# First expert block: order of fetches, routing steps and one-hots

## The chip, the cores and the metric

The kernel runs on one core of a Trainium2 chip. The metric is the device time of one execution in microseconds (us); what is given for the kernel before is the median of three timed runs.

## The reference

Attention with a sigmoid in place of the softmax, then a mixture of experts with one expert per token and a skip rule, then a dense two-layer network, all in float32:

```python
# q, k, v: (4, 12, 448, 64)
scores = np.matmul(q, k.transpose(0, 1, 3, 2)) / np.sqrt(64) - np.log(448)
x = np.matmul(1 / (1 + np.exp(-scores)), v)      # then (1792, 768): token, 12 heads * 64
# experts: w_skip (768), w_gate (768, 8), w1 (8, 768, 1024), w2 (8, 1024, 768)
run = x @ w_skip > 0                             # the other tokens pass unchanged
e_idx = np.argmax(x[run] @ w_gate, axis=1)
gate_w = softmax(x[run] @ w_gate)[e_idx]
x[run] += gate_w * (np.maximum(x[run] @ w1[e_idx], 0) @ w2[e_idx])
# dense: w_in (768, 2048), w_out (2048, 768)
h = x @ w_in
out = np.where(h > 0, h, np.exp(np.minimum(h, 0)) - 1) @ w_out
```

## The kernel before

**Products.** A float32 factor is kept as a high and a low part: ScalarE (ACT) casts the high part, VectorE (DVE) subtracts it to get the low part, and `gemm` makes three matmuls of the two pairs. For weights `split_w` does this, the cast `whi` on ACT and the subtraction `wlo` on DVE, 128 x 1536 at a time.

**Stages.** Attention goes in 24 steps of two heads (`scores` and mixing, matmuls `ps` and `po`) and leaves x transposed in `xT`. The experts work on blocks of 256 tokens; which tokens stand in a block is data. Block 0 is special: its tokens come from the first ten 128-row tiles alone (SOON = 10), so that its routing (`sooner`) is done during the last attention steps. Its rows are gathered from the copy of x in DRAM, `x_d`, by two indirect DMAs of GpSimd (`gather_first`), 128 rows each, as soon as the slot table `inv` has been turned into `slot_0`. Blocks 1 and on wait for the routing of all 14 tiles.

**Block 0's weights.** An expert's weights are 8 chunks of 768 KB, c0 to c3 of w1 and c4 to c7 of w2. `fetch` issues them on the SP queue, which runs in program order: c0 and c1 one step before the end of attention, c2 and c3 when the last step begins, c4 and c5 right behind attention, c6 and c7 when c0 and c1 have been split, since they take their buffers (NRAW0 = 6). Two chunks at a time are held as split pairs ahead of use: `ahead(i, c)` splits chunk c + 2.

**The product of block 0.** `first_block` is one generator-driven program. `columns` flips the gathered rows on TensorE (PE) and splits them into `x2` (`both` in the trace). Then come 16 calls of `up_one(0, c, f)`, chunk c (0 to 3) and column group f (0 to 3), which build h; after c = 1 and c = 3 `h_one` makes h's high part on ACT and its low part on DVE. After each `up_one` the generator `routing` is advanced by one step, up to its next `yield`; this is how the routing of the last four tiles and the order of all further blocks are woven into block 0's products. Chunks c4 to c7 follow (`back`), with four routing steps after each, then `slot_order`, twelve small matmuls that use twelve `one_hot` tiles and the offsets `ca`.

**The late row tiles.** The first steps of `routing` also write the last four tiles of x to `x_d`: `rows(t)` for t = LATE to LATE + 3 (10 to 13). Each has six flips on PE into two PSUM banks (always the same two, `acc2` and `acc4`), two ACT copies into a row buffer `xr`, and one write on the SP queue. There are two buffers `xr`, so the copies of one tile need the write of the tile two before it, and the flips of the next tile need the banks that these copies read.

**The routing chain.** After the late tiles' choices (`choose`, `positions`) DVE computes the first slot of every expert, every token's slot, one-hots of slots (`rt_tok`, in `spots`), and block kinds. PE multiplies these: `ordered` and `inv` (which gives `slot_tok`, by which block 1 is gathered), `kn` and `ig`; then DVE makes `kinds`, from which PE loads the branch of block 1, and the twelve one-hots (`order_rows`).

What sets the order on each engine is the order in which these Python functions issue the instructions; engines run in program order and meet through semaphores.

Of the kernel before, what the change touches and what calls it, by code (L numbers as in the profile page):

```python
# [91 lines left out]
def build(nc, tc, a):  # L92
# [3 lines left out]
    with ExitStack() as top:  # L96
# [80 lines left out]
        with ExitStack() as st:  # L177
# [250 lines left out]
            def sooner():  # L428
# [55 lines left out]
                gather_first()  # L484

            whi_t, wlo_t = [], []

# [8 lines left out]
            def raw_of(i, c):  # L496
                return raw_t[(8 * i + c) % NRAW if i else c % NRAW0]

            def fetch(i, chunks):
                if i == NB:  # L500
                    return
                e = nc.values_load(
                    blk_e[i : i + 1, :1] if i else blk_0[:1],
                    engines=[mybir.EngineType.SP], min_val=0, max_val=E - 1,
                )
                for c in chunks:
                    src = (w1, w2)[c // 4][bass.ds(e, 1), c % 4].rearrange("o p f -> (o p) f")
                    nc.sync.dma_start(raw_of(i, c), src)

            def gather(i, late=True):  # L510
                at = slot_ext if late else slot_tok
                for h in range(2):
# [7 lines left out]
                    )  # L520

            def gather_first():
                for h in range(2):
                    nc.gpsimd.indirect_dma_start(
                        out=xg_t[0][h][:],
                        out_offset=None,
                        in_=x_d[: SOON * P, :],
                        in_offset=bass.IndirectOffsetOnAxis(ap=slot_0[:, h : h + 1], axis=0),
                        bounds_check=SOON * P - 1,
                        oob_is_err=False,  # L530
                    )

# [84 lines left out]
            for n in range(steps + 1):  # L617
# [5 lines left out]
                if n == steps:  # L623
                    qst.close()
                    wi1p = top.enter_context(tc.tile_pool(name="wi1p", reuse_waits="tile", bufs=1))
                    wi1 = wi1p.tile([P, DM], F32, name="wi1")
                    tokp = st.enter_context(tc.tile_pool(name="tokp", reuse_waits="tile", bufs=1))
                    some_weights(tokp, 2, 2)
                    fetch(0, range(2, 4))
                    lg = logits(B - 1, None, range(KD - 2))  # L630
# [59 lines left out]
            assert done_rows == LATE and narrowed == 2 * FA  # L690
            columns(0, [pss.tile([P, 2, 512], F32, name="pc", tag="ps")[:, 0] for _ in range(3)])
            logits(B - 1, lg, range(KD - 2, KD))
            ast.close()
# [38 lines left out]
            def routing():  # L732
# [9 lines left out]
                yield  # L742
                rows(LATE + 1, banks)
                pos, cnt = positions(SOON, NTT, acc_t[5])
                nc.vector.scalar_tensor_tensor(
                    ni, cnt, float(BLK - 1), took[:, 0], op0=ALU.add, op1=ALU.subtract
# [13 lines left out]
                nc.vector.reduce_sum(span[:, 0], tmp, axis=AX.X)  # L760
                yield
                rows(LATE + 2, banks)
                nc.vector.scalar_tensor_tensor(
# [3 lines left out]
                nc.vector.reduce_sum(fv, fo, axis=AX.X)  # L767
                yield
                rows(LATE + 3, banks)
                run(places(SOON, NTT, pos))  # L770
                nc.gpsimd.tensor_add(posk[:, late], posv[:, late], skip[:, late])
                yield
# [6 lines left out]
                    aa, sa.to_broadcast([P, NTT, NHB]), grid("iota_a", NTT, NHB), op=ALU.is_equal  # L779
                )  # L780
                yield
                run(spots(SOON, NTT, slot_i[:, late]))
                yield
                nc.vector.tensor_add(span[:, 1], span[:, 0], nb[:, 0])
# [4 lines left out]
                with nc.allow_low_precision("whole numbers up to 14"):  # L789
                    nc.vector.reduce_sum(blk_e, own, axis=AX.XY)  # L790
                yield
                ordered = acc_t[2][:, :E1]
# [184 lines left out]
            def first_block(aside):  # L977

                for c in range(4):
                    nh, c3 = divmod(c, 2)  # L980
                    for f in range(4):
                        up_one(0, c, f)
                        next(aside, None)
                        if c3:
                            h_one(4 * nh + f)
                        if f == 2:
                            ahead(0, c)
                ahead(0, 4)
                for c in range(4, 8):
                    if c == 5:  # L990
                        ahead(0, 5)
                    back(0, 1, P, range(c, c + 1))
                    for _ in range(4):
                        next(aside, None)
                outcome(0, 1, P)
                run(aside)
                back(0, 0, P, range(4, 5))
                slot_order()
# [142 lines left out]
            def order_rows():  # L1141
                for t in range(NOR):
                    nc.vector.tensor_scalar(
                        one_hot[0][:, t], iota_h, cr[:, t], None, op0=ALU.is_equal
                    )
# [310 lines left out]
```

## Time and profile before

| | |
|---|---|
| median of three runs | 918.95 us (917.61 to 919.28) |
| profiled execution, its own time | 919.79 us |
| its span, first to last instruction | 918.0 us |
| PE (matmul) busy | 887.1 us, 97% |
| DVE busy | 557.7 us, 61% |
| ACT busy | 485.3 us, 53% |
| POOL (GpSimd) busy | 75.6 us, 8% |
| DMA engines, mean rate | 147 GB/s |

The busy times are sums over the whole span. Time outside the span (919.79 - 918.0) is start and end of the program. The block that is changed lies from about 160 to 215 us of the span.

### The profile page before, as it was taken

The numbers are of one execution on the slowest core, as the hardware profiler recorded it, in microseconds if no ns is written. First come the engines' busy times: TensorE is split into PE (matmuls) and PEld (weight loads), VectorE is DVE, ScalarE is ACT, GpSimd is POOL, SyncE is SP. The second block draws the span as 40 slices with busy tenths as digits, with TensorE's granted clock in tenths as the row PEclk, the third lists the DMA queues.
The fourth block names the chain that finished last, engine by engine and source line by source line (L and its number), as shares of the span: only waits on it lengthen the run. The fifth ranks groups of instructions, "written<-read, shape, count | busy, mean of one in ns | idle before, by whom it ended". The sixth has DMA issues, their size and how long they took to land.

```text
span 918.0 us, 13615 instructions
## 1 busy us (share of the span) xinstructions
PE 887.1 (97%) x5208; PEld 714.6 (78%) x5208; DVE 557.7 (61%) x872; ACT 485.3 (53%) x679; POOL 75.6 (8%) x76
## 2 busy tenths in 40 slices
PE   9999999889999897999899999999999999999998
PEld 4445545589999786888688888888888888888997
DVE  2968678478566375786688886533443543443664
ACT  7777776453455463674445544444443444444664
POOL 1000000113101032221100000100000100000100
PEclk9999999999999999899999999999999999999999
DMA  8788875659947084964553431100100100000100
GB/s 286 253 278 281 297 268 208 262 163 411 391 159 278 13 318 179 409 221 145 203 160 87 123 115 41 69 1 1 35 18 18 69 1 1 0 1 10 61 1 35
DMA packets 34196, 134.73 MB, mean 147 GB/s; under 512 B 4698, under 2 KB 5850, under 8 KB 34098
## 3 DMA queue, kind: packets, MB, share of 16 engines
q1 hardware_dynamic: 29474, 114.22, 35.0%
q0 software_dynamic: 4480, 19.01, 5.8%
q8 instruction: 57, 0.93, 0.4%
q14 instruction: 41, 0.34, 0.1%
q10 hardware_dynamic: 144, 0.23, 0.1%
HBM read 112.47 MB, written 23.99 MB: 149 GB/s over the span
## 4 chain that ended last, share of the span: by engine, by line
PE 91%; DVE 3%; ACT 2%; issue 2%; DMA 1%; POOL 0%; DVEq 0%; ACTq 0%; POOLq 0%
PE acc L1331 16%; PE pt L1331 10%; PE acc L1298 8%; PE acc L1299 8%; PE acc L1300 8%; PE po L256 8%; PE ps L242 7%; PE acc L549 5%; PE acc L548 5%; PE acc L550 5%; PE acc L142 1%; PE acc L907 1%; PE acc L908 1%; DVE wlo L541 1%; PE pt L142 1%
## 5 line engine op out<-in xcount | busy, mean ns | idle before, releaser
L541 DVE TENSOR_TENSOR wlo<-raw,whi 128x1536 fp32r<-128x1536 f32 x64 | 111.3, 1756 | 31.8 <-ACT whi L539 31.2
L1307 ACT ACTIVATE m<-acc 128x512 f32<-128x512 f32 (+1 forms) x64 | 34.9, 545 | 177.2 <-PE acc L1300 167.0
L1309 DVE SCALAR_TENSOR_TENSOR m<-m,acc 128x512 f32<-128x512 f32 (+1 forms) x64 | 39.8, 621 | 143.7 <-ACT m L1308 143.7
L539 ACT CAST whi<-raw 128x1536 fp32r<-128x1536 f32 x64 | 93.8, 1481 | 21.8 <-PE acc L550 8.8
L249 ACT ACTIVATE at<-ps,bias 112x896 f32<-112x896 f32 x96 | 88.9, 1011 | 24.9 <-PE ps L242 24.5
L1331 PE MATMUL acc<-wol,gh 128*128 128x256 f32 x320 | 100.7, 315 | 0.0
L1331 PE MATMUL acc<-woh,gl 128*128 128x256 f32 x320 | 100.4, 314 | 0.0
L1331 PE MATMUL acc<-woh,gh 128*128 128x256 f32 x320 | 100.4, 314 | 0.0
L1299 PE MATMUL acc<-x,wih 128*128 128x512 f32 (+1 forms) x270 | 96.2, 356 | 0.0
L1298 PE MATMUL acc<-x,wih 128*128 128x512 f32 (+1 forms) x270 | 96.2, 356 | 0.0
L1300 PE MATMUL acc<-x,wil 128*128 128x512 f32 (+1 forms) x270 | 96.1, 356 | 0.0
L549 PE MATMUL acc<-wlo,both 128*128 128x384 f32 (+1 forms) x236 | 84.0, 356 | 4.1 <-issue 3.7
L548 PE MATMUL acc<-whi,both 128*128 128x384 f32 (+1 forms) x236 | 84.8, 359 | 0.0
L550 PE MATMUL acc<-whi,both 128*128 128x384 f32 (+1 forms) x236 | 83.5, 354 | 0.0
L256 PE MATMUL po<-at,vt 112*64 112x448 f32 x384 | 77.5, 545 | 0.0
L1287 DVE TENSOR_TENSOR wol<-wo,woh 128x768 fp32r<-128x768 f32 x64 | 61.2, 957 | 23.3 <-ACT woh L1286 23.0
L1331 PEld LDWEIGHTS acc<-woh,gh 128*128 128x128 f32 x320 | 60.3, 188 | 9.9
L1331 PEld LDWEIGHTS acc<-wol,gh 128*128 128x128 f32 x320 | 60.3, 188 | 9.4
L1286 ACT CAST woh<-wo 128x768 fp32r<-128x768 f32 x64 | 53.3, 833 | 25.9 <-PE acc L1331 25.8
L1313 DVE TENSOR_TENSOR gl<-m,gh 128x512 fp32r<-128x512 f32 (+1 forms) x64 | 40.1, 626 | 40.5 <-ACT gh L1312 40.5
L1331 PEld LDWEIGHTS acc<-woh,gl 128*128 128x128 f32 x320 | 60.1, 188 | 4.2
L1281 DVE TENSOR_TENSOR wil<-wi,wih 128x768 fp32r<-128x768 f32 x60 | 57.4, 957 | 6.7 <-ACT wih L1280 6.0
(261 smaller groups left out, 1876.0 us busy)
## 6 DMA issues: line engine op xcount, KB each, us to landing
raw<-in_w SPq DMA_DIRECT2D x66, 768.0 KB, 7.9
raw<-in_wi SPq DMA_DIRECT2D x9, 768.0 KB, 6.3
raw<-in_wo SPq DMA_DIRECT2D x9, 768.0 KB, 6.8
vt<-in_v SPq DMA_DIRECT2D x12, 448.0 KB, 5.4
x_d<-xr SPq DMA_DIRECT2D x14, 384.0 KB, 5.4
raw<-in_wi SPq DMA_DIRECT2D x14, 384.0 KB, 3.1
raw<-in_wo SPq DMA_DIRECT2D x14, 384.0 KB, 3.1
qr<-in_q SPq DMA_DIRECT2D x11, 448.0 KB, 4.8
```

The costliest lines, as they stand in the source:

```text
L242: nc.tensor.matmul(ps[:CP, j, :S], kk[head, p, c * CP : (c + 1) * CP], qq[head, p], start=(i == 0), stop=(i == 2),)
L249: nc.scalar.activation(at[:, :, c, :], ps[:CP, :, :S], AF.Sigmoid, bias=bias[:CP], scale=QK_SCALE)
L256: nc.tensor.matmul(po[64 * j : 64 * j + 64, :S], vt[:, 2 * (hp % 2) + j, c, :], at[:, j, c, :], start=(c == 0), stop=(c == NCH - 1),)
L539: nc.scalar.copy(w_hi, raw)
L541: nc.vector.tensor_sub(w_lo, raw, w_hi)
L548: nc.tensor.matmul(o, a_hi, b_hi, start=first, stop=False)
L549: nc.tensor.matmul(o, a_hi, b_lo, start=False, stop=False)
L550: nc.tensor.matmul(o, a_lo, b_hi, start=False, stop=last)
L1298: nc.tensor.matmul(o, a, b, start=(cc == 0), stop=False)
L1299: nc.tensor.matmul(o, a, c, start=False, stop=False)
L1300: nc.tensor.matmul(o, wil[:, cc], b, start=False, stop=(cc == KD - 1))
L1331: nc.tensor.matmul(o, a, b, start=(clears and f == 0 and k_ == 0), stop=(f == KF2 - 1 and k_ == 2), skip_group_check=True,)
```

## The change

Six edits. `fetch` of c2 and c3 gets a dependency on both gathers of `gather_first`. A one-element Exp on ACT stands behind `columns` (the function table for Exp is loaded there). The steps of `routing` are regrouped: DVE work moves to earlier steps, `rows(LATE + 1)` to `rows(LATE + 3)` stand later within their step, and two steps fewer are left ahead of `ordered`. The splits of c2 to c5 are issued behind `up_one` (1, 0), (1, 2), (2, 2) and (3, 2), where they were issued behind (0, 2), (1, 2), (2, 2) and (3, 2). The twelve `one_hot` instructions go from DVE to GpSimd. The load of the dense weights `wi1`, whose line is unchanged, comes out at another place.

```diff
@@ -483,6 +483,9 @@
                 nc.vector.tensor_scalar_add(slot_0, inv, float(NT))
                 gather_first()
 
+            SYNC = mybir.DependencyInfo(
+                mybir.DependencyClass.Sync, mybir.DependencyReason.DATA
+            )
             whi_t, wlo_t = [], []
 
             def some_weights(pool, raws, splits):
@@ -496,7 +499,7 @@
             def raw_of(i, c):
                 return raw_t[(8 * i + c) % NRAW if i else c % NRAW0]
 
-            def fetch(i, chunks):
+            def fetch(i, chunks, after=()):
                 if i == NB:
                     return
                 e = nc.values_load(
@@ -505,7 +508,9 @@
                 )
                 for c in chunks:
                     src = (w1, w2)[c // 4][bass.ds(e, 1), c % 4].rearrange("o p f -> (o p) f")
-                    nc.sync.dma_start(raw_of(i, c), src)
+                    dma = nc.sync.dma_start(raw_of(i, c), src)
+                    for other in after:
+                        tc.add_manual_dep(dma.ins, other.ins.name, SYNC)
 
             def gather(i, late=True):
                 at = slot_ext if late else slot_tok
@@ -519,16 +524,18 @@
                         ),
                     )
 
+            first_rows = []
+
             def gather_first():
                 for h in range(2):
-                    nc.gpsimd.indirect_dma_start(
+                    first_rows.append(nc.gpsimd.indirect_dma_start(
                         out=xg_t[0][h][:],
                         out_offset=None,
                         in_=x_d[: SOON * P, :],
                         in_offset=bass.IndirectOffsetOnAxis(ap=slot_0[:, h : h + 1], axis=0),
                         bounds_check=SOON * P - 1,
                         oob_is_err=False,
-                    )
+                    ))
 
             def split_w(i, c, hi=True, lo=True):
                 if i == NB:
@@ -626,7 +633,7 @@
                     wi1 = wi1p.tile([P, DM], F32, name="wi1")
                     tokp = st.enter_context(tc.tile_pool(name="tokp", reuse_waits="tile", bufs=1))
                     some_weights(tokp, 2, 2)
-                    fetch(0, range(2, 4))
+                    fetch(0, range(2, 4), first_rows)
                     lg = logits(B - 1, None, range(KD - 2))
                 if p == 0 and n < steps:
                     if n:
@@ -689,6 +696,7 @@
             run(soon)
             assert done_rows == LATE and narrowed == 2 * FA
             columns(0, [pss.tile([P, 2, 512], F32, name="pc", tag="ps")[:, 0] for _ in range(3)])
+            nc.scalar.activation(warm, bias, AF.Exp)
             logits(B - 1, lg, range(KD - 2, KD))
             ast.close()
             pst.close()
@@ -740,8 +748,9 @@
                 fetch(0, range(NRAW0, 8))
                 rows(LATE, banks)
                 yield
-                rows(LATE + 1, banks)
                 pos, cnt = positions(SOON, NTT, acc_t[5])
+                run(places(SOON, NTT, pos))
+                nc.gpsimd.tensor_add(posk[:, late], posv[:, late], skip[:, late])
                 nc.vector.scalar_tensor_tensor(
                     ni, cnt, float(BLK - 1), took[:, 0], op0=ALU.add, op1=ALU.subtract
                 )
@@ -758,17 +767,12 @@
                 )
                 nc.vector.tensor_mul(tmp, nb.to_broadcast([P, E, E]), first)
                 nc.vector.reduce_sum(span[:, 0], tmp, axis=AX.X)
-                yield
-                rows(LATE + 2, banks)
                 nc.vector.scalar_tensor_tensor(
                     base[:, 0], span[:, 0], float(BLK), took[:, 0], op0=ALU.mult, op1=ALU.subtract
                 )
                 nc.vector.tensor_mul(fo, base.to_broadcast(sh), oh)
                 nc.vector.reduce_sum(fv, fo, axis=AX.X)
-                yield
-                rows(LATE + 3, banks)
-                run(places(SOON, NTT, pos))
-                nc.gpsimd.tensor_add(posk[:, late], posv[:, late], skip[:, late])
+                rows(LATE + 1, banks)
                 yield
                 nc.vector.scalar_tensor_tensor(
                     s1, fv, float(BLK), later_in, op0=ALU.add, op1=ALU.mult
@@ -778,9 +782,9 @@
                 nc.vector.tensor_tensor(
                     aa, sa.to_broadcast([P, NTT, NHB]), grid("iota_a", NTT, NHB), op=ALU.is_equal
                 )
+                rows(LATE + 2, banks)
                 yield
                 run(spots(SOON, NTT, slot_i[:, late]))
-                yield
                 nc.vector.tensor_add(span[:, 1], span[:, 0], nb[:, 0])
                 nc.vector.scalar_tensor_tensor(
                     own, span, con("row"), con("ramp").rearrange("p (j e) -> p j e", e=E),
@@ -788,6 +792,8 @@
                 )
                 with nc.allow_low_precision("whole numbers up to 14"):
                     nc.vector.reduce_sum(blk_e, own, axis=AX.XY)
+                rows(LATE + 3, banks)
+                yield
                 yield
                 ordered = acc_t[2][:, :E1]
                 counted = [per[:, 0], *(oh1[:, t] for t in range(SOON, NOR))]
@@ -976,6 +982,7 @@
 
             def first_block(aside):
 
+                turns = [(1, 0), (1, 2), (2, 2), (3, 2)]
                 for c in range(4):
                     nh, c3 = divmod(c, 2)
                     for f in range(4):
@@ -983,8 +990,8 @@
                         next(aside, None)
                         if c3:
                             h_one(4 * nh + f)
-                        if f == 2:
-                            ahead(0, c)
+                        if (c, f) in turns:
+                            ahead(0, turns.index((c, f)))
                 ahead(0, 4)
                 for c in range(4, 8):
                     if c == 5:
@@ -1140,7 +1147,7 @@
 
             def order_rows():
                 for t in range(NOR):
-                    nc.vector.tensor_scalar(
+                    nc.gpsimd.tensor_scalar(
                         one_hot[0][:, t], iota_h, cr[:, t], None, op0=ALU.is_equal
                     )
 
```

The SP queue, before: the chunks c2 to c7 (`raw2`, `raw3` of w1; `raw4`, `raw5`, `raw0`, `raw1` of w2), `wi1`, and the writes of the late tiles to `x_d` (the first is r10's).

```order
L508 DMA raw3_1837<-in_w1 128x1536
L714 DMA wi1_1828<-wi_d1_62 128x768
...
L508 DMA raw5_1917<-in_w2 128x1536
L508 ISA
L508 DMA raw0_106<-in_w2 128x1536
L297 DMA x_d_60<-xr_2000 128x768
L508 ISA
L508 DMA raw1_107<-in_w2 128x1536
L297 DMA x_d_60<-xr_2019 128x768
L297 DMA x_d_60<-xr_2054 128x768
L297 DMA x_d_60<-xr_2076 128x768
```

The same place of the SP queue, of the change:

```order
L722 DMA wi1_1828<-wi_d1_62 128x768
L511 ISA
L511 DMA raw2_1836<-in_w1 128x1536
...
L511 DMA raw5_1918<-in_w2 128x1536
L511 ISA
L511 DMA raw0_106<-in_w2 128x1536
L511 ISA
L511 DMA raw1_107<-in_w2 128x1536
L297 DMA x_d_60<-xr_2001 128x768
L297 DMA x_d_60<-xr_2040 128x768
```

`wi1` went from behind c3 to ahead of c2, and r10's write from between c6 and c7 to behind c7.

ACT, before, from r11's copies (`xr_2019`) to the split of c3: the copies of the late tiles, the cast of c2 (`whi2` from `raw2`) and h's high parts (`both` from `acc`).

```order
L296 COPY xr_2019<-acc2_1905 128x384
L296 COPY xr_2019<-acc4_1907 128x384
L539 CAST whi2_1912<-raw2_1836 128x1536
L296 COPY xr_2054<-acc2_1905 128x384
...
L296 COPY xr_2076<-acc4_1907 128x384
L931 ACTIVATE both_117<-acc0_1903 128x256
L931 ACTIVATE both_117<-acc1_1904 128x256
L931 ACTIVATE both_117<-acc3_1906 128x256
L539 CAST whi3_1914<-raw3_1837 128x1536
```

ACT, of the change, from the last cast of `columns` to the split of c3:

```order
L570 CAST both_117<-pc_1870 128x512
L699 ACT_TABLE_LOAD
L699 ACTIVATE warm_200<-bias_80 128x1
L296 COPY xr_2001<-acc2_1906 128x384
...
L296 COPY xr_2063<-acc2_1906 128x384
...
L296 COPY xr_2091<-acc4_1908 128x384
L937 ACTIVATE both_117<-acc0_1904 128x256
L546 CAST whi2_1913<-raw2_1836 128x1536
L937 ACTIVATE both_117<-acc1_1905 128x256
L937 ACTIVATE both_117<-acc3_1907 128x256
L546 CAST whi3_1915<-raw3_1837 128x1536
```

The table load and the one-element Exp are new; the cast of c2 went from ahead of r12's copies (`xr_2054`, now `xr_2063`) to behind r13's and behind h's first high part.

DVE, before, around `kinds`: the low part of c4 (`wlo0` from `raw4`), the gate values (`val`, `gr`, `av`), two of h's low parts (`both` from `pt1` and `acc0`) and `kinds`.

```order
L541 TENSOR_TENSOR wlo0_1833<-raw4_1916,whi0_1832 128x1536
L816 CAST val_1954<-gw_1952 128x14
L817 TENSOR_TENSOR gr_1953<-gw_1952,val_1954 128x14
L818 TENSOR_SCALAR val_1954<-gr_1953 128x14
L821 TENSOR_TENSOR av_1955<-aa_1948,val_1954 128x840
L932 SCALAR_TENSOR_TENSOR both_117<-pt1_1902,both_117 128x256
L932 SCALAR_TENSOR_TENSOR both_117<-acc0_1903,both_117 128x256
L835 TENSOR_TENSOR kinds_99<-acc2_1905,taken_1949 1x15
```

DVE, of the change, the same instructions:

```order
L822 CAST val_1955<-gw_1953 128x14
L823 TENSOR_TENSOR gr_1954<-gw_1953,val_1955 128x14
L824 TENSOR_SCALAR val_1955<-gr_1954 128x14
L827 TENSOR_TENSOR av_1956<-aa_1949,val_1955 128x840
L548 TENSOR_TENSOR wlo0_1833<-raw4_1917,whi0_1832 128x1536
L841 TENSOR_TENSOR kinds_99<-acc2_1906,taken_1950 1x15
```

`kinds` now stands right behind the low part of c4, with the gate values ahead of it, and ahead of the last low parts of h.

## Rows read from the trace of the kernel before

**Rows 1.** Windows of 5 us: busy by engine, PE clock, DMA share, GB/s

```profile
170.00:175.00 5.00, 1.46 (x7) 1.27 (x8) 0.16 (x1) 0.20 (x1) 0.00 (x0) 0.89 1.01 400
205.00:210.00 5.00, 4.93 (x27) 4.22 (x25) 4.89 (x9) 1.73 (x2) 0.00 (x0) 1.00 1.02 416
```

**Rows 2.** Timeline of POOL and PE, 163 to 178: start, us, instruction, idle before

```profile
164.92 1.00 POOL L524 DMA_INDIRECT xg<-x_d,slot  x1 [0.31 <-issue]
...
166.26 3.23 PE L256 MATMUL po<-at,vt 112*64 112x448 f32 x16
...
173.87 2.61 PE L142 MATMUL pc<-cst,xg 128*128 128x128 f32 x11 [2.91 <-DMA xg<-x_d,slot]
...
177.69 0.39 PE L548 MATMUL acc<-both,whi 128*128 128x256 f32 x1
```

**Rows 3.** DMA issues of block 1's gathers, 197 to 200: us to landing

```profile
xg<-x_d,slot_tok POOLq DMA_INDIRECT x1, 4.0
...
xg<-x_d,slot_tok POOLq DMA_INDIRECT x1, 4.7
```

**Rows 4.** Timeline of PE, landmarks from 185 to 215

```profile
185.72 0.49 PE L142 MATMUL acc<-cst,xT 128*128 128x128 f32 x3
...
189.47 0.28 PE L548 MATMUL pt<-both,whi 128*128 128x256 f32 x1
...
191.69 0.41 PE L801 MATMUL acc<-aa,rt_tok 128*128 128x30 f16 x10
...
193.36 0.36 PE L548 MATMUL acc<-both,whi 128*128 128x256 f32 x1
...
214.43 0.46 PE L1151 MATMUL acc<-ca,one_hot 128*128 128x12 f16 x12
```

**Rows 5.** Costliest groups: instruction, count, busy and mean ns, idle before, releaser

```profile
L541 DVE TENSOR_TENSOR wlo<-raw,whi 128x1536 fp32r<-128x1536 f32 x64 | 111.3, 1756 | 31.8 <-ACT whi L539 31.2
...
L539 ACT CAST whi<-raw 128x1536 fp32r<-128x1536 f32 x64 | 93.8, 1481 | 21.8 <-PE acc L550 8.8
```

**Rows 6.** Windows, two stretches of low clock

```profile
173.87:177.28 3.41, 3.41 (x15) 2.39 (x15) 1.54 (x3) 1.76 (x3) 0.00 (x0) 0.50 0.64 263
365.00:371.80 6.80, 5.33 (x14) 4.25 (x14) 2.41 (x3) 2.08 (x2) 2.35 (x3) 0.50 1.00 402
```

**Rows 7.** Timeline of SP and ACT, DMA issues of r10's and r11's writes

```profile
182.81 0.33 SPq L508 DMA_DIRECT2D raw<-in_w  x1
...
x_d<-xr SPq DMA_DIRECT2D x1, 384.0 KB, 2.4
...
x_d<-xr SPq DMA_DIRECT2D x1, 384.0 KB, 5.2
...
188.83 0.86 ACT L296 COPY xr<-acc 128x384 f32<-128x384 f32 x2 [3.21 <-DMA x_d<-xr]
```

**Rows 8.** Timeline of SP, and the DMA issue of c6's fetch at 170.20

```profile
161.78 0.35 SPq L508 DMA_DIRECT2D raw<-in_w  x1
...
170.20 0.33 SPq L508 DMA_DIRECT2D raw<-in_w  x1
...
raw<-in_w SPq DMA_DIRECT2D x1, 768.0 KB, 7.9
```

**Rows 9.** Waits of PE, 176 to 215: us in total, times, longest

```profile
PE pt L548 <- DVE both L932: 1.5, 1, 1.5
PE pt L548 <- DVE kinds L835: 0.6, 1, 0.6
```

**Rows 10.** Lines of POOL; timeline of DVE, 209 to 215

```profile
L464 POOL TENSOR_TENSOR posk<-posv,skip 128x10 f32<-128x10 f32 x1 | 0.6, 602 | 4.5 <-DVE posv L411 4.5
...
L592 POOL CAST iota_h<-early_cst 128x128 f16<-128x128 f32 x1 | 0.3, 292 | 0.0
...
L771 POOL TENSOR_TENSOR posk<-posv,skip 128x4 f32<-128x4 f32 x1 | 0.2, 205 | 7.6 <-DVE posv L411 7.6
...
210.61 0.17 DVE L1123 CAST cr<-hf 128x12 f32<-128x12 int32 x1
```

## The prediction

> Names: c2 to c7 are the third to eighth weight chunk of block 0, r10 to r13 the four late 128-row tiles (`rows(LATE)` to `rows(LATE + 3)`), up(c,f) one call of `up_one(0, c, f)`.
>
> **What bounds the kernel now.** I read the busy time by window first, then the timeline there, then the waits. Between 170 and 175 us TensorE is busy 1.46 of 5 us while the DMA engines are full (share 1.01) [rows 1]: the one long hole near the change. The timeline says why: the last attention matmul ends at 166.26 + 3.23 = 169.49, the flips of block 0's gathered rows go on at 173.87, the first product starts at 177.69 [rows 2]. The second gather was issued at 164.92 and took nearly 9 us beside weight chunks; block 1's two gathers, with nothing else in flight, landed 4.0 and 4.7 us after issue [rows 3]. Later landmarks on TensorE: r13's flips at 185.72, up(2,0) at 189.47, `slot_order` at 214.43 [rows 4]. From there TensorE's program is the same, so I price the change by when `slot_order` starts; what follows shifts with it.
>
> **The gathers go alone: 5.3 us early.** c2 and c3 now wait for both gathers, and SP works in order, so c4 to c7 wait too. The second gather lands at 164.92 + 4.7 = 169.6, when TensorE comes free. Ahead of the first product then stand four flips (three take 0.49 [rows 4], so 0.6), one ACT cast and one VectorE subtraction of 512 columns; a third of the 1536-column ones, 1.48 / 3 and 1.76 / 3 [rows 5], gives 0.5 and 0.6. Products start near 171.5 instead of 177.69; the half clock from 173.87 to 177.28 [rows 6] goes with the hole. From first product to r13's flips took 185.72 - 177.69 = 8.0 us; I add 0.9, since the copy of lgT, for which the token flips wait, stands behind three such subtractions, which no longer have slow flips between them. TensorE is at r13's flips at 180.4, 5.3 early. Bounds for the gather: 4.0 or 8.9 us; at 8.9 nothing is gained here.
>
> **c2 to c7 pass the row writes: TensorE waits 6.0 us.** On SP r10's write now stands behind c7, where before it stood ahead of it. ACT's copy of r12 needs r10's buffer (there are two), so it waits until r10's write has landed, and r13's flips need the banks that this copy frees. Before, the same wait came one tile later and was shorter: r13's copy sat 3.21 us for r11's write, which was behind c7 and landed 5.2 us after issue; r10's, alone, took 2.4 [rows 7]. How late is r10 now? Before, from c2's issue at 161.78 to c6's landing at 170.20 + 7.9 = 178.1 [rows 8], 16.3 us, went five chunks, wi1 and the two gathers: 5 x 768 + 384 + 768 = 4992 KB, with the engines full (1.01 between 170 and 175 [rows 1]). Now c2 is issued near 169.7, and up to r10's landing go six chunks and r10 itself: 6 x 768 + 384 = 4992 KB, the same amount. So r10 lands near 169.7 + 16.3 = 186.0. (c7 waits for the low part of c1. It was issued at 182.81 [rows 7], 5.1 behind the first product; now that is 171.5 + 0.9 + 5.1 = 177.5, before the queue has run dry.) Lower bound: 5.11 MB at the 416 GB/s of 205 to 210 [rows 1] are 12.3 us, plus what r10 alone needed beyond its bytes, 2.4 - 0.9 = 1.5: 183.5. I take 186.0, a measured run of the same load. TensorE gets to r13's flips after the first half of r12's copy, at 186.4: 0.7 later than before.
>
> The Trainium skill ("DMA: Bandwidth & Descriptors", section "Anatomy of one DMA") gives a DMA about 2.0 us plus its bytes over 436 GB/s; as an estimate from that page, 4992 KB take 13.7 us, r10 lands at 183.4 and the sum below would be 2.6 lower, -2.0. This trace's 16.3 us for the same bytes disagrees.
>
> **The splits come later: 1.15 us.** c2's cast stood ahead of r12's copy on ACT; now it stands behind r13's copies and h's first high part. From 186.4: the rest of r12's copy and r13's (held to r11's landing, 0.9 after r10's) to 187.9, the high part 0.4 (256 columns), c2's cast 1.5, its low part on VectorE 1.8 [rows 5]: 191.5. up(2,0) needs that low part in its third matmul, so it starts near 191.3 against 189.47, 1.83 late. TensorE's own work to that point ends about then too: before 189.47 - 185.72 = 3.75, and now `ordered` and `inv`, some 0.8, as well: 191.0.
>
> **The routing chain ahead of h's low parts: 1.65 us back.** Before, up(2,0) to `slot_order` took 214.43 - 189.47 = 24.96. `inv`, 191.69 to 193.36 with its wait for rt_tok [rows 4], now lies ahead of up(2,0), and rt_tok is ready long before: -1.65. The wait of 1.5 for h's fourth low part [rows 9] shrinks to 0.3, since no routing work stands in front of it: -1.2. But `kinds` now stands behind c4's low part (1.76) on VectorE, and TensorE loads it after up(3,0), so its wait of 0.6 [rows 9] becomes 1.8: +1.2. The low parts of c5 to c7 follow as before. So 23.3, and `slot_order` would start at 191.3 + 23.3 = 214.6. The early Exp table load costs nothing: ACT has nothing to do between the column casts and r10's copy, about 2 us; without that cover it is one cast's worth.
>
> **One-hots on GpSimd: 0.1 us.** They can start when `cr` is cast; before that was at 210.61 [rows 10], 3.8 ahead of `slot_order`, and now two small steps fewer stand between c7's low part and it: some 4.0 ahead. No such GpSimd instruction is in the trace. Nearest from below: its 128x128 cast to f16, 0.292. Its small tensor_tensor takes 0.205 alone and 0.602 in the one place where it started beside a wide VectorE instruction [rows 10]; half of that excess on each of the twelve, 0.292 + 0.2, is my upper bound, 0.5. I take 0.33, near the cast: 12 x 0.33 = 4.0 just fits, 0.1 beyond for the start. At 0.5 they take 6.0 and `slot_order` is 2.0 later. What VectorE is rid of lies behind the last low part; TensorE waits for none of it.
>
> **The clock: 0.3 us.** After the hole from 169.5 the granted clock was 0.50 from 173.87 to 177.28; another such stretch lasts from 365.0 to 371.8 [rows 6]. A hole of 6 us should bring one again: 3.4 to 5 us at half speed behind 186.4 delay TensorE by 1.7 to 2.5, but the waits for c2's low part, for h's fourth and for `kinds` take most of it in; 0.3 to 1.2 is left. I take 0.3.
>
> Sum, against the profiled execution's 919.79: -5.3 + 6.0 + 1.15 - 1.65 + 0.1 + 0.3 = +0.6. The median of the runs shown, 918.95, lies 0.84 below that execution, so I forecast 918.95 + 0.6 = about 919.5. About 0.2% (1.84 us) is what a measurement here can tell from no change.
>
> **Rivals.**
> 1. *The queue drains at its full rate.* r10 lands at the bound, 183.5, and all behind it comes 2.5 earlier, with little half clock: +0.6 - 2.5 - 0.3 = -2.2, 916.7. For it: 416 GB/s are sustained later, and no gather is mixed in. Against: the engines were full in those 16.3 us too.
> 2. *The row writes hold nobody,* because a write gets through beside queued reads. Then -5.3 - 1.65 + 0.1 = -6.9, 912. For it: nothing but the separate direction. Against: r11's 5.2 us behind c7.
> 3. *Slower: the one-hots take 0.45 to 0.5 each.* `slot_order` stands behind them, and from 0.34 on each further 0.1 costs 1.2: +0.6 + 1.3 to 2.0, 920.9 to 921.6. For it: GpSimd's 0.602 against 0.205. Against: the wide low parts of this block are over when the one-hots begin. The Trainium skill ("Advanced Engine Details and Errata", section "GPSIMD Details") says that GpSimd shares a read and a write interface with VectorE and conflicts with its two-port or two-input instructions. The 0.602 agrees that there is a conflict.
> 4. *Slower: half clock for 6.8 us,* as after 365.0 [rows 6]: 1.7 more on TensorE with no wait left to take it in, +2.3, 921.2.
> 5. *Slower: the gather alone is as slow as before.* c2 to c7 are then issued 4.2 later, and r10 lands near 190: +4.8, 923.7. Against: 4.0 and 4.7 for the same form [rows 3].
>
> **How the numbers follow.** Forecast 0.48 (its own range 917.1 to 920.8), rival 1 0.18, rival 2 0.08, rival 3 0.16, rival 4 0.07, rival 5 0.03. Faster is 1 and 2, 0.26; slower 3 to 5, 0.26; same 0.48. The range runs from rival 1 with one-hots of 0.29 (916.3) to rival 3's upper end with half a microsecond of more half clock (922.1); outside lie rivals 2 and 5 and a little of 3 and 4, under 0.2.
>
> **What would show it.** In the changed profile: the second gather landing about 4.7 after issue and no half clock at 174; products from about 171.5; ACT waiting 5 to 6 us for an x_d write in r12's copy; TensorE idle from about 180.4 to 186.4 with a stretch at 0.5 behind it; `kinds` behind c4's low part; one-hots of about 0.33 on GpSimd for which TensorE hardly waits. I am wrong towards faster if r10's write lands before 184, towards slower if the one-hots exceed 0.4 each or the low clock lasts.

## The result and the profile after

The change is slower: 926.07 us median of 5 runs (924.34 to 928.44) against 919.28 of 5 runs of the kernel before (917.61 to 922.96); ratio 1.0067, 95% interval [1.0038, 1.0096]. The forecast was 919.5 in a range of 916.3 to 922.1, so the time lies outside it, by 4 us.

The profiled execution took 924.34 us with a span of 922.5, against 919.79 and 918.0. It is the shortest of the five, so its trace explains 4.5 us and not all of the 6.2 that the ratio says; the rest is taken up below. Its attention happened to end 0.48 us earlier (at 169.01 instead of 169.49); the table doesn't correct for that.

| TensorE reaches | before | forecast | after |
|---|---|---|---|
| first product of block 0 | 177.69 | 171.5 | 172.26 |
| r13's flips | 185.72 | 186.4 | 186.68 |
| up(2,0) | 189.47 | 191.3 | 192.51 |
| first matmul of `slot_order` | 214.43 | 215.0 | 215.13 |
| flips of block 1, right behind `slot_order` | 214.75 | 215.4 | 218.73 |

The timeline of TensorE in the changed kernel shows these places (compare [rows 2, 4]):

```profile
170.03 1.42 PE L142 MATMUL pc<-cst,xg 128*128 128x128 f32 x11 [0.76 <-DMA xg<-x_d,slot]
...
172.26 0.39 PE L555 MATMUL acc<-both,whi 128*128 128x256 f32 x1
...
186.68 1.54 PE L142 MATMUL acc<-cst,xT 128*128 128x128 f32 x6 [5.91 <-ACT xr L296]
...
192.51 0.36 PE L555 MATMUL pt<-both,whi 128*128 128x256 f32 x1
...
215.13 0.55 PE L1158 MATMUL acc<-ca,one_hot 128*128 128x12 f16 x7
216.07 0.18 PE L1158 MATMUL acc<-ca,one_hot 128*128 128x12 f16 x1 [0.40 <-POOL one_hot L1150]
...
218.38 0.18 PE L1158 MATMUL acc<-ca,one_hot 128*128 128x12 f16 x1 [0.40 <-POOL one_hot L1150]
218.73 0.54 PE L142 MATMUL pt<-cst,xg 128*128 128x128 f32 x3 [0.17 <-issue]
```

Up to 215.13 the change cost 0.7 us, as forecast. There TensorE starts the twelve matmuls, gets seven one-hots with hardly a wait, and then takes one every 0.58 us. The timeline of POOL shows all twelve in one row (compare [rows 10]):

```profile
211.25 7.07 POOL L1150 TENSOR_SCALAR one_hot<-iota_h,cr 128x128 f16<-128x128 f16 x12 [13.40 <-DVE hf L1132]
```

The waits of TensorE, 160 to 222, the three largest (compare [rows 9]):

```profile
PE acc L142 <- ACT xr L296: 5.9, 1, 5.9
PE acc L1158 <- POOL one_hot L1150: 2.0, 5, 0.4
PE acc L555 <- DVE kinds L841: 1.6, 1, 1.6
```

The waits list 2.0 us for the one-hots, but five short matmuls stand between those waits: the stretch from 215.13 to 218.73 takes 3.60, and took 0.32 before (214.75 - 214.43). So the one-hots cost 3.28. Counted from the end of attention, block 1's flips are 3.98 + 0.48 = 4.46 later. From them to the end of the span it takes 703.77 us, against 703.25 before: the tail is 0.52 longer, about as much as attention happened to give, and so the span is 4.5 longer.

### The profile page after: what moved, and what is told of

The parts are those of the page before. It is cut to its first block, busy times and chain, and to the rows that moved or that the text cites. A ratio compares the mean times of both kernels' runs of the same rounds, so it can differ in the third digit from the quotient of the medians.

```text
span 922.5 us, 13617 instructions
## 1 busy us (share of the span) xinstructions
PE 888.1 (96%) x5208; PEld 715.8 (78%) x5208; DVE 556.3 (60%) x860; ACT 485.3 (53%) x680; POOL 82.4 (9%) x88
## 4 chain that ended last, share of the span: by engine, by line
PE 87%; DMA 4%; DVE 3%; ACT 2%; issue 1%; POOL 1%; SPq 0%; ACTq 0%; DVEq 0%; POOLq 0%
PE acc L1338 16%; PE pt L1338 10%; PE acc L1305 8%; PE acc L1306 8%; PE acc L1307 8%; PE po L256 7%; PE ps L242 6%; PE acc L555 5%; PE acc L556 5%; PE acc L557 5%; DMA raw<-in_w 2%; PE acc L142 2%; DVE wlo L548 1%; PE acc L913 1%; PE acc L914 1%
## 5 line engine op out<-in xcount | busy, mean ns | idle before, releaser
L1294 DVE TENSOR_TENSOR wol<-wo,woh 128x768 fp32r<-128x768 f32 x64 | 61.2, 957 | 23.3 <-ACT woh L1293 22.9
```

The lines of the kernel that those rows point to most:

```text
L1294: nc.vector.tensor_sub(pair[1], wo_r[f], pair[0])
```

## The experiments

All ratios are to the kernel before, run beside them on the same chip. The experiments ran on several chips, so medians of different experiments compare only roughly. Line numbers shift by a few where an experiment adds lines.

**1 and 2. The one-hots, undone and alone.** First the change with them back on VectorE, then the kernel before with them on GpSimd:

```diff
-                    nc.gpsimd.tensor_scalar(
+                    nc.vector.tensor_scalar(
                         one_hot[0][:, t], iota_h, cr[:, t], None, op0=ALU.is_equal
```

> The change with its twelve one-hots back on VectorE. Theory A (what made the change slower is GpSimd's 0.59 us per one-hot: 7.07 us for twelve from 211.25, TensorE held to 218.4): the first matmul of slot_order stays near 215.1, the twelve need no wait, block 1's flips start near 215.5 instead of 218.73, and the profiled time is 3.3 us below the change's 924.34, so 921.0, some 1 to 2 us above the kernel before. Theory B (the loss lies in the row write behind c7 and the low clock behind it, and the one-hots only fill a wait that would be there anyway): no more than 0.5 us less, 924.

> The kernel before with only the one-hots moved to GpSimd. Theory A: cr is cast at 210.6 there, twelve at 0.59 end at 217.9, block 1's flips start near 218.0 instead of 214.75, and the time is 3.2 us above the kernel before, ratio 1.0035. Theory B: within 0.5 us of the kernel before. If each one-hot is longer than 0.59 here, because VectorE works beside them, contention has a share; if it is 0.58 to 0.60, it has none.

Undone: ratio 1.0014 [0.9994, 1.0033], profiled 920.25. On VectorE a one-hot takes 0.25 us, and `slot_order` runs through, as its lines (busy, mean ns, idle before) and its timeline show:

```profile
L1150 DVE TENSOR_SCALAR one_hot<-iota_h,cr 128x128 f16<-128x128 f16 x12 | 2.0, 250 | 0.0
```

```profile
214.59 0.46 PE L1158 MATMUL acc<-ca,one_hot 128*128 128x12 f16 x12
```

Alone: ratio 1.0061 [1.0038, 1.0083], and the median 4.5 us above. Theory A holds in both directions, theory B in neither: nearly all of the loss comes with the one-hots. Alone they cost more than the 3.2 us expected. Its profiled execution is one of the three longest of the twelve (929.65 to 930.22, mean granted clock 0.982 or 0.983); the other nine took 922.58 to 927.43, at 0.986 to 0.993. Its `slot_order` ends at 219.9. The windows around and behind that show what was added there (after the busy times of the engines come granted clock, DMA share, GB/s):

```profile
218.90:222.00 3.10, 2.32 (x11) 2.15 (x12) 1.62 (x8) 0.59 (x1) 0.75 (x2) 0.53 1.03 420
222.00:226.00 4.00, 4.00 (x16) 4.00 (x15) 3.00 (x4) 2.54 (x3) 2.92 (x3) 0.51 1.02 416
226.00:228.00 2.00, 2.00 (x14) 2.00 (x13) 0.67 (x2) 1.51 (x2) 1.61 (x2) 1.00 1.02 412
```

The half clock (1.2 of 2.4 GHz) from 219.9 to 226 is another 2.9 us of TensorE's work (2.1 x 0.47 + 4.0 x 0.49). In the change's own profile that clock stays at 1.00 (215.13 to 260), so this is not in its 4.5 us. Its other four executions, 0.6 to 4.1 us longer, left no trace, but their mean granted clock is on record. 2.9 us of lost work in 922.5 would take 0.003 off the profiled execution's 0.990. Only the longest, 928.44 us at 0.987, is that low; the others, 924.90, 926.07 and 926.36, have 0.990, 0.989 and 0.991. So for most of them a half clock of that length is not the reason.

**3. What a GpSimd one-hot costs.** Each is made in two halves of 64 columns; then, in the kernel of experiment 6, scratch instructions of four forms on the idle GpSimd.

```diff
-                    nc.gpsimd.tensor_scalar(
-                        one_hot[0][:, t], iota_h, cr[:, t], None, op0=ALU.is_equal
-                    )
+                    for s in (slice(0, P // 2), slice(P // 2, P)):
+                        nc.gpsimd.tensor_scalar(
+                            one_hot[0][:, t, s], iota_h[:, s], cr[:, t], None, op0=ALU.is_equal
+                        )
```

> The change with every one-hot made by two GpSimd instructions of 64 columns. If the 0.59 us are work per element, an instruction takes about 0.3 to 0.33 and the 24 together still 7 to 8 us, the time within 1 us of the change. If they are a fixed cost of an instruction, each takes over 0.5, the 24 some 13 us, and the time is some 6 us above the change.

```diff
+                for _ in range(3):
+                    nc.gpsimd.tensor_copy(probe, iota_h)
+                    nc.gpsimd.tensor_scalar(probe, iota_h, 5.0, None, op0=ALU.is_equal)
+                    nc.gpsimd.tensor_scalar(probe, iota_h, cr[:, 0], None, op0=ALU.is_equal)
+                    nc.gpsimd.tensor_scalar(probe, iota_h, cr[:, 0], None, op0=ALU.mult)
```

> The kernel with kinds ahead of c4's low part, and on GpSimd, idle there, three times four instructions of 128x128 f16 into a scratch tile that nobody reads: a copy, a compare with a constant, a compare with a scalar per partition (the one-hot's form), a multiplication by it. Theory A1 (the form is what costs: a compare or a scalar operand is dearer than a copy): copy near 0.29, the compare with a scalar per partition 0.59. Theory A2 (an f16 input costs more than the float32 one of the cast in the kernel before): all four near 0.55 to 0.6. The time says nothing: the scratch work takes some 6 us of GpSimd, which ends ahead of its next gather.

Halves: the lines of POOL give a mean of 450 ns and a median of 446, beside 590 for a whole one in experiment 2, so neither limb is right: as an estimate from these two sizes, about 2.25 ns a column ((590 - 446) / 64) on some 0.30 us per instruction. The 24 took 10.1 us, the one execution 932.26. Forms, in the timeline of POOL:

```profile
205.94 0.76 POOL L1159 TENSOR_SCALAR probe<-iota_h,cr 128x128 f16<-128x128 f16 x1
206.78 0.61 POOL L1160 TENSOR_SCALAR probe<-iota_h,cr 128x128 f16<-128x128 f16 x1
207.46 0.29 POOL L1157 COPY probe<-iota_h 128x128 f16<-128x128 f16 x1
207.84 0.53 POOL L1158 TENSOR_SCALAR probe<-iota_h 128x128 f16<-128x128 f16 x1
208.46 0.60 POOL L1159 TENSOR_SCALAR probe<-iota_h,cr 128x128 f16<-128x128 f16 x1
```

A1 holds: a copy takes 0.29, a compare 0.53 with a constant and 0.60 with a scalar per partition, as does the multiplication. The f16 input is not what is dear.

The other two compares with a scalar took 0.72 and 0.76, while VectorE had small instructions beside them (the second is the first line above). A wide one beside it costs far more. The first compare with a constant, earlier in the same trace, took 2.03 instead of 0.53; here it is in the timeline of all engines with the subtraction on VectorE that was running when it started:

```profile
193.97 1.76 DVE L551 TENSOR_TENSOR wlo<-raw,whi 128x1536 fp32r<-128x1536 f32 x1 [0.46 <-ACT whi L549]
...
194.10 2.03 POOL L1158 TENSOR_SCALAR probe<-iota_h 128x128 f16<-128x128 f16 x1
```

It ended 0.40 us behind the subtraction, as if it had been held through it. It was also the first compare of this size in the trace, so this row alone does not exclude a cost of first use; the last section has a row that does not share that doubt.

**4. The row writes.** One-hots on VectorE, and r12 and r13 get two row buffers of their own, so that no ACT copy waits for a write; the writes stay behind c7. Then, with two buffers again, the late writes go on ScalarE's queue.

```diff
+            rowl = []
             def rows(t, banks=None):
-                xr = rowp.tile([P, DM], F32, name="xr")
+                pool = rowp if t < LATE + 2 else rowl[0]
+                xr = pool.tile([P, DM], F32, name="xr")
...
+            rowl.append(xst.enter_context(tc.tile_pool(name="rowl", bufs=2, side="right")))
```

> The change with one-hots on VectorE and two more row buffers for r12 and r13, so that their ACT copies need no write to have landed; the writes themselves stay behind c7 on SP. Theory A (the 5.9 us wait at r13's flips and the low clock behind it take back what the lone gathers gave): the flips of r13 start near 180.6 instead of 186.68, no clock of 0.5 behind them, up(2,0) near 185 instead of 192.51, slot_order 6 to 7.5 us earlier than in the run with one-hots on VectorE alone, the time near 914, ratio 0.994 to 0.996. Rival C (with that wait gone the splits or the weight chunks are late: c2 to c7 all land only by 186): TensorE waits for low parts instead, and 2 us or less are gained.

```diff
-                nc.sync.dma_start(x_d[t * P : (t + 1) * P, :], xr)
+                queue = nc.scalar if t >= LATE else nc.sync
+                queue.dma_start(x_d[t * P : (t + 1) * P, :], xr)
```

> The change with one-hots on VectorE, two row buffers as in the change, and the late tiles' writes issued from the queue of ScalarE instead of SP's. Theory A1 (a write stands behind all the bytes that are queued when it is issued, whatever its queue): r10's write, issued near 176.7, still lands near 186, TensorE waits 5.8 us at r13's flips, the time is that of the run with one-hots on VectorE alone, ratio 1.001. Theory A2 (what held it was its place on SP's queue behind c7; the DMA engines serve both queues in turn): it lands 2.5 to 5 us after issue, the wait at r13's flips shrinks to 0 to 2 us, ratio 0.993 to 0.997.

Four buffers: ratio 0.9935 [0.9914, 0.9955], median 914.92, faster than both kernels. In its timeline of TensorE r13's flips wait for nothing and `slot_order` starts 6.5 us earlier than in experiment 1 (214.59):

```profile
180.57 0.82 PE L142 MATMUL acc<-cst,xT 128*128 128x128 f32 x6
...
208.06 0.46 PE L1163 MATMUL acc<-ca,one_hot 128*128 128x12 f16 x12
```

The clock there is 1.00 throughout, and no low part of the weights makes TensorE wait longer than 0.4. Rival C falls.

On ScalarE's queue: ratio 1.0009 [0.9991, 1.0027], not to be told from experiment 1. Here is its timeline of ACT and PE:

```profile
177.47 0.33 ACTq L298 DMA_DIRECT2D x_d<-xr  x1
...
184.73 0.86 ACT L296 COPY xr<-acc 128x384 f32<-128x384 f32 x2 [5.34 <-DMA x_d<-xr]
...
185.27 1.54 PE L142 MATMUL acc<-cst,xT 128*128 128x128 f32 x6 [3.69 <-ACT xr L296]
```

And its DMA queues (packets, MB, share of the engines), the first row from 179 to 181, the other two from 181 to 183; q1 is SP's, q10 ScalarE's:

```profile
q1 hardware_dynamic: 133, 0.72, 101.8%
...
q1 hardware_dynamic: 90, 0.54, 66.7%
q10 hardware_dynamic: 83, 0.25, 31.4%
```

The truth lies between A1 and A2: r10's write moved nothing until 181, and then got about a third of the engines. It freed the buffer at 184.7, some 7.3 us after issue, against 7.8 from SP's queue. The wait at the flips shrank from 5.8 to 3.7 us, and the half clock behind it stayed (0.50 from 185 to 190).

**5. The lone gathers, undone.** The four-buffer kernel with `fetch(0, range(2, 4))`, without the dependency.

> The four-buffer kernel without the dependency of c2 and c3 on the gathers (wi1 and r10's write go back to where they stood on SP before). Theory A (the lone gathers are worth what the product starts earlier, and nothing behind it takes it in once the row buffers are there): the second gather takes 8 to 9 us again, products start near 177.7 instead of 172.3, with a stretch at clock 0.5 before them, and slot_order follows 5 to 5.5 us later than in the four-buffer kernel: the time is 5 to 6 us above its 914.92, ratio to the kernel before 0.999 to 1.0005. Rival (the late chunks c2 to c7 cost the four-buffer kernel something that comes back here): 3 us above or less.

Ratio 1.0003 [0.9987, 1.0019], median 919.76. Its gathers land late again, products start at 177.06 instead of 172.23, `slot_order` at 212.67 instead of 208.06, and the clock dips again (0.79 from 175 to 180). So the lone gathers are worth some 5 us (4.6 at `slot_order` in these two traces, 0.7% by the two ratios), once nothing behind takes them in.

**6. `kinds` ahead of c4's low part,** in the four-buffer kernel:

```diff
-                turns = [(1, 0), (1, 2), (2, 2), (3, 2)]
+                turns = [(1, 0), (1, 2), (3, 0), (3, 2)]
```

> The four-buffer kernel with the split of c4 issued behind up(3,0) instead of up(2,2), so that kinds stands ahead of c4's low part on VectorE. Theory A (the 1.7 us that TensorE waits for kinds are one low part, 1.75): the wait goes, and slot_order and the time come 1.5 to 1.7 us earlier, 913.3, ratio 0.992. Rival: c4's and c5's low parts, each later, become a wait of the same size ahead of back(c4) or back(c5), and the time stays within 0.5 us.

Ratio 0.9923 [0.9901, 0.9944]. The wait for `kinds` (1.7) is gone from the list. From first product to `slot_order` it takes 207.55 - 173.10 = 34.45 us, against 208.06 - 172.23 = 35.83: 1.4 less, as theory A has it. The ratios alone, 0.9923 and 0.9935, can't tell the two kernels apart.

**7. Without the early Exp,** the four-buffer kernel without `nc.scalar.activation(warm, bias, AF.Exp)`.

> The four-buffer kernel without the early Exp: its table load, 1.28 us, then stands ahead of the Exp of the routing on ScalarE, near 185. If the early load is free and worth something, TensorE waits up to 1.3 us more here for h's low parts or c4's split, up to 916.2. If ScalarE has room there, the time is within 0.5 us of the four-buffer kernel's 914.92.

Ratio 0.9951 [0.9931, 0.997], which overlaps with 0.9935. The load (1.28 us) stands at 186.22, TensorE waits for the same things as with the early load, and from first product to `slot_order` it takes 35.85 us. The edit is worth nothing here.

**8. Two things alone:** the kernel before with the dependency of c2 and c3 and the two row buffers.

> The kernel before with two things alone: c2 and c3 wait for the gathers, and r12 and r13 have row buffers of their own. The routing steps, the splits, the Exp and the one-hots stand as before. Theory A (these two make nearly all of what the four-buffer kernel gained, the regrouped routing some 1.2 us: from r13's flips to slot_order the kernel before took 214.43 - 185.72 = 28.7, the four-buffer kernel 208.06 - 180.57 = 27.5): r13's flips near 180.6, slot_order near 209.3, ratio to the kernel before 0.9945 to 0.996. Rival (the regrouped routing is worth nothing in the end, or is needed so that the splits come in time): ratio 0.9935 or, on the other side, above 0.997.

Ratio 0.9903 [0.9883, 0.9923], median 913.09. With 0.9923 of experiment 6, whose interval overlaps, this is the best that ran. From first product to `slot_order` it takes 206.44 - 171.76 = 34.68 us, 1.15 less than the four-buffer kernel with the regrouped routing, so theory A was wrong by its sign. The rival's first limb, that the regrouping is worth nothing, is right, though its ratio, 0.9935, lies above the interval. The two kernels also differ in the splits and the early Exp; the Exp is worth nothing (experiment 7). The waits say where the four-buffer kernel loses: `kinds` costs 0.7 here and 1.7 there. That is the place of c4's split more than the routing steps: with `kinds` ahead of c4's low part (experiment 6) the regrouped program takes 34.45, 0.23 less than here.

```profile
PE pt L558 <- DVE kinds L847: 0.7, 1, 0.7
PE acc L559 <- issue: 0.3, 1, 0.3
PE acc L559 <- DVE wlo L551: 0.3, 1, 0.3
PE pt L558 <- DVE both L944: 0.2, 1, 0.2
```

## Why the prediction was wrong

**The step that failed: "One-hots on GpSimd: 0.1 us".** The term measured 3.28. The one-hots started where the forecast had them (211.25, 3.9 ahead of `slot_order`), but each took 0.59, not 0.33, and also more than the upper bound of 0.5. The price was taken from a cast [rows 10], and a copy does take 0.29; a compare takes twice that (experiment 3). The bound asked how much to add to the cast for a conflict with VectorE, which it read from two small additions, 0.602 against 0.205. The rows bear the conflict out. In the timeline of the kernel before, the slow addition ends 0.07 us behind a VectorE instruction that started just ahead of it:

```profile
155.14 0.55 DVE L166 TENSOR_SCALAR mg<-mf 128x768 int32<-128x768 int32 x1
155.16 0.60 POOL L464 TENSOR_TENSOR posk<-posv,skip 128x10 f32<-128x10 f32 x1 [4.52 <-DVE posv L411]
```

But it is not what made the one-hots slow: VectorE had nothing longer than 0.62 us beside them, and the last five, with VectorE idle, still came every 0.58. Rival 3 had the right place and too low a price, and its mechanism was not the cause: by its own slope (1.2 us for each 0.1 above 0.34), 0.59 would have given +0.6 + 3.0 in the trace. No row of the kernel before had the form at this size. Its trace had two compares with a constant on GpSimd, 0.53 us for ten columns and 0.24 for four; the 0.53 (139.50 to 140.03) also ends just behind a VectorE instruction of 0.55 (139.33 to 139.88), so it prices the conflict and not the compare. The form had no price there, and the bound of 0.5 was a guess.

With 3.28 in place of 0.1 the forecast would have been 922.7, 3.4 below the measured 926.07. In the two traces 0.2 of that is the sum up to `slot_order` (+0.70 against +0.5) and 0.5 the longer tail. The other 2.6 are differences between executions: the forecast put the median 0.84 below the profiled execution of the kernel before, and that of the change lies 1.73 above its profiled one. The lower end of the range doesn't follow from its own terms either: one-hots of 0.29 give back at most the 0.1 of that term, which makes 916.6 and not 916.3.

The Trainium skill ("GPSIMD Engine Reference", section "4.1 Engine selection") sends elementwise work to VectorE and calls one-input operations on GpSimd roughly line-rate. The advice agrees with these runs, 0.25 against 0.59 per one-hot; "line-rate" doesn't for a compare of 128 columns, which took 2.4 times as long as on VectorE.

**The terms up to `slot_order`: a sum that came right in part by luck.** The gathers gave 4.95 (forecast 5.3; 0.48 of it is attention's earlier end), the wait for the write cost 5.91 (6.0), splits and clock 2.08 (1.45), the routing chain gave 2.34 (1.65). The last two errors cancel.

**Lone gathers: right, a little large.** The second gather landed near 170.0 (forecast 169.6) and the hole and its half clock went. Products started 5.4 earlier instead of 6.2, partly because the token logits' matmuls (0.9 us) also stand ahead of them.

**c2 to c7 past the row writes: right.** The DMA issue of r10's write (us to landing), and the timeline of SP and ACT with the copy of r12 that waited for it:

```profile
x_d<-xr SPq DMA_DIRECT2D x1, 384.0 KB, 7.8
```

```profile
178.22 0.42 SPq L297 DMA_DIRECT2D x_d<-xr  x1
...
186.14 0.86 ACT L296 COPY xr<-acc 128x384 f32<-128x384 f32 x2 [7.51 <-DMA x_d<-xr]
```

It landed at 186.0, the forecast figure, and TensorE waited 5.91 us (forecast 6.0). c2 was issued at 170.19 and not 169.7, so the same bytes took 15.8 us instead of 16.3; these half microseconds cancel by luck. So the bytes in the queue at the rate of the stretch before priced it, not the full rate of rival 1. That rate was there for a while, 410 GB/s from 172 to 181; from 182 to 184 the engines, still full, moved 237. Why is open. The estimate by the Trainium skill, 183.4, was 2.6 early; the section that the prediction quotes for it describes DMAs issued by GpSimd, and SP issued these. Rival 2 is excluded for the change, and experiment 4 shows what it would have given.

**Splits 1.15, clock 0.3: the sum near (2.08 against 1.45), the parts not.** The window behind the start of r13's flips:

```profile
186.68:189.91 3.23, 3.23 (x15) 3.23 (x16) 0.42 (x1) 2.46 (x5) 0.00 (x0) 0.50 0.41 164
```

3.2 us at half clock cost 1.6, and since they delayed TensorE to 192.51, up(2,0) did not wait for c2's low part at all. The forecast let the waits take the clock in; here the clock took in the wait. Up(2,0) came 5.83 behind r13's flips, where it came 3.75 behind them before (forecast 4.9): 1.6 of the 2.08 are the clock, 0.46 are `ordered` and `inv`, now ahead of it.

**Routing chain: right in this program, wrong as a gain.** From up(2,0) to `slot_order` it took 22.62 (forecast 23.3), with the wait for `kinds` at 1.6 (forecast 1.8). But experiment 8 shows that the old order is 1.15 us shorter over the whole block once the row writes hold nobody, and experiment 6 that this is mostly the price of `kinds` behind c4's low part.

**Early Exp: right,** it costs nothing, and brings nothing either.

**What stays open:** the ratio says 6.2 us and the trace 4.5 (924.34 / 919.79 = 1.0049, inside the interval). Experiments 1 and 2 give 0.5 to 0.6% for the one-hots, about 5 us, where the trace shows 3.28. A half clock behind that wait, as seen in experiment 2, fits the mean clock of one of the change's five executions (928.44 us); what made the other three longer than the profiled one is not shown.

## What to carry to other kernels

Price an instruction on GpSimd by a row of the same form, not by a copy of the same size, and where no such row exists put the upper bound well above twice the copy; twelve in a row ahead of a waiting matmul multiply the error. When reads are held back to let a short transfer go alone, list the writes that will queue behind them and who needs their buffers: here a hole of 6 us came back 11 us further down the program. With 6 KB more of buffers per partition the ratio was 0.9935 (the rest of the change, one-hots on VectorE) or 0.9903 (these two edits alone), without them 1.0014. A wait on the busiest engine may cost more than its length, since a stretch at half clock can follow it (3.2 us behind the wait of 5.9 here).

## What the runs showed of the hardware

A second DMA queue gave a 384 KB write no quick passage: issued at 177.47, while weight chunks filled the engines, it moved nothing until 181 and then shared them about one to two. The Trainium skill ("DMA: Bandwidth & Descriptors", section "Queues, rings and completion order") says that an engine alternates between the queues that have work; the sharing from 181 on agrees, and the 3.5 us before it are not explained by it.

A GpSimd instruction can stand still while VectorE works beside it. Beside a VectorE instruction of 0.55 us an addition of ten columns took 0.60, beside one of 1.76 a compare took 2.03 instead of 0.53; the first ended 0.07 us behind the VectorE instruction, the second 0.40. The clearest case is one cast of one column (`kmax_i`): in the trace of the four-buffer kernel it took 0.94 and ended 0.04 us behind the second of two VectorE instructions in a row (149.28 to 150.33); in the other eleven traces it took 0.45 or 0.46, and in that of the kernel before it ended 0.05 behind the first of the two. So a GpSimd row with VectorE busy beside it gives a wait and not a price.
